# Binding attention matmuls behind the feed-forward column in front of them, in a fused attention and two-layer feed-forward kernel

## The chip, the cores and the metric

The kernel runs on one core of a Trainium2 chip. The metric is the device time of one execution in microseconds (us); lower is better. A core has five engines that run their own instruction queues in order and wait for each other through semaphores: TensorE (PE, matrix products; its weight loads are listed as PEld), VectorE (DVE), ScalarE (ACT), GpSimd (POOL) and SyncE (SP). SP and POOL here mostly issue DMA transfers.

## The reference, cut to what matters

Attention with a memory term over 4 batches, 8 heads, 576 positions of 64, then two feed-forward (FFN) layers over the 2304 tokens, 512 to 2048 to 512 each, all in float32:

```python
scores = q @ k.T / 8, causal          # per batch and head
local  = softmax(scores) @ v
mem    = (phi(q) @ M_prev) / (phi(q) @ z_prev + 1e-6)      # phi(x) = elu(x) + 1
x = g * mem + (1 - g) * local         # g from beta, heads joined: 2304 x 512
x = softplus(x @ w1_in) @ w1_out      # layer 0
x = elu(x @ w2_in) @ w2_out           # layer 1
```

## The kernel before, in words

**FFN.** The 2304 tokens are cut into five chunks of 512, 512, 448, 416 and 416 (`CHUNKS`), each made of parts of one or two batches. `ffn(c, layer)` handles one chunk in one layer, as a generator with 32 yields. Its first half, the in half, makes 16 columns of 128 hidden units: 12 matmuls each (L675 to L677: four slices of the model width, each with a high and a low part of weights and input), then a chain of ScalarE and VectorE instructions (`act`, L679, L680) that ends in a tile g with a high and a low part. Four PSUM banks (tag h) hold columns whose chain is not yet done. Its second half, the out half, makes 4 output tiles in 4 quarters each: 16 steps of 12 matmuls (L691 to L693) that read the g tiles. I write (c, layer) for such a stage, so (1,0) is chunk 1 in layer 0; a stage has 384 matmuls of its own. "Column" below also means a quarter of the out half.

**Attention.** `attention(b, part)` is a generator too. Part A covers positions 0 to 255 of a batch (two heads at once), part B the rest (head by head). A head of part B goes through scores (L344, L356), the maximum (DVE L333), the exponential (ACT L337), scaling (ACT L384), transposes through the PE (L410, and L302 for the memory term), copies that split them into high and low parts (ACT L420, DVE L421), and the gather, a chain of matmuls into one bank (L453, L457, L459, L460). L453 stands once per head, so the L453s count the heads; there are 32 heads in part B. A chunk of FFN can only start when its batches' attention is done.

**Weights.** All four weight matrices arrive in 64-bit form and are converted on the chip (`convert`): a raw load into a buffer of tag big (three of them, shared with the head loads qk of attention), ACT L605, DVE L606 and L607, ACT L97, DVE L616, and a save to DRAM (L584), from where later chunks load them (L635). The generator `conversions` does part of those of layer 1 ahead of time; the rest are made when the column that needs them first comes up. The first use of the output weights of layer 1 is in the out half of (0,1).

**What sets the order.** `TUNE["order"]` lists the stages. For each it has two pairs, for the in half and for the out half: how many attention steps and how many conversions are called per column. `next(side)` calls one attention step, inside `tc.high_priority(offset=400)`. A scheduler then sorts all instructions by priority and by a timeline that it models, under their dependencies, and fixes the order on each engine when the kernel is built. With the high priority it may place the instructions of a step ahead of columns that were called before that step. The loop with `next(side, None)` at L786 to L791 is where the change is made.

Of the kernel before, what the change touches and what calls it, by code (L numbers as in the profile page):

```python
# [18 lines left out]
KD = DM // 128  # L19
KF = DFF // 128  # L20
# [19 lines left out]
    hi='ssss ssss', lo='v', sc='vv ssv',  # L40


    order=((0, 0, (1.6, 0.0), (0.6, 0.2)), (1, 0, (0.1, 0.2), (0.5, 0.6)), (0, 1, (0.7, 0.0), (0.8, 0.0)), (1, 1, (0.8, 0.0), (1.1, 0.0)), (2, 0, (0.3, 0.0), (0.8, 0.0)), (2, 1, (0.5, 0.0), (0.8, 0.0)), (3, 0, (0.3, 0.0), (0.8, 0.0)), (3, 1, (0.5, 0.0), (0.8, 0.0)), (4, 0, (0.0, 0.0), (0.0, 0.0)), (4, 1, (0.0, 0.0), (0.0, 0.0))),
)


# [12 lines left out]
def kernel(  # L59
# [15 lines left out]
    ve, se, ge, te = nc.vector, nc.scalar, nc.gpsimd, nc.tensor  # L75
# [16 lines left out]
    def f32(ap):  # L92
        return ap.bitcast(F32)

    def copy(eng, dst, src):
        if eng is se:
            se.copy(dst, src)  # L97
        else:
            eng.tensor_copy(dst, src)
# [37 lines left out]
    def x(c, k):  # L137
        return slots[SLOT[c]][k]
# [2 lines left out]
        for t in sph:  # L141
            ge.memset(t[:, SOFF[4] + S:], 0.0)

    gates = []
    busy = [set() for _ in CHUNKS]

    def into(b, k, c0, src):
# [474 lines left out]
    def weights(src, key):  # L622
        if key in made:
            w = made.pop(key)
            with tc.issue_after(raw_loads[count - 1]):
                save(key, w)
        else:
            with tc.high_priority(offset=T["pri"][key in scratch]):
                w = make(src, key)
        return w[:, 0], w[:, 1]  # L630
# [18 lines left out]
    def act(c, layer, t, h):  # L649
        if layer == 0:  # L650
            se.activation(t, h, ACTF.Abs)
            se.activation(t, t, ACTF.Exp, scale=-1.0)
            se.activation(t, t, ACTF.Ln, bias=ones)  # L653
            ve.scalar_tensor_tensor(t, h, 0.0, t, ALU.max, ALU.add)  # L654
        elif c == 0:
            se.activation(t, h, ACTF.Relu, scale=-1.0)
            se.activation(t, t, ACTF.Exp, scale=-1.0)
            ve.scalar_tensor_tensor(t, t, -1.0, h, ALU.add, ALU.max)
        else:
            ve.tensor_scalar(t, h, 0.0, None, ALU.min)  # L660
            se.activation(t, t, ACTF.Exp)  # L661
            ve.scalar_tensor_tensor(t, t, -1.0, h, ALU.add, ALU.max)  # L662

    def ffn(c, layer):
        win, wout = ((w1i, w1o), (w2i, w2o))[layer]
        N = WIDTH[c]
        gs = []
        for f in range(KF):
            hi, lo = weights(win[f], f"{layer}i{f}")
            t = two.tile([128, 512], F32, name="t", tag="t")  # L670
            g = gp.tile([128, 2, 512], F32R, name="g", tag="g")
            h = psf.tile([128, 512], F32, name="h", tag="h")
            for k in range(KD):
                xk = x(c, k)
                te.matmul(h[:, :N], hi[:, k, :], xk[:, 0, :N], start=k == 0, stop=False)  # L675
                te.matmul(h[:, :N], hi[:, k, :], xk[:, 1, :N], start=False, stop=False)  # L676
                te.matmul(h[:, :N], lo[:, k, :], xk[:, 0, :N], start=False, stop=k == KD - 1)  # L677
            act(c, layer, t[:, :N], h[:, :N])
            se.copy(g[:, 0, :N], t[:, :N])  # L679
            ve.tensor_sub(g[:, 1, :N], t[:, :N], f32(g)[:, 0, :N])  # L680
            gs.append(g)
            if layer and f == KF - 1:
                busy[c].add("in")
            yield
        for d in range(KD):
            h = psf.tile([128, 512], F32, name="h", tag="h")
            for u in range(4):
                hi, lo = weights(wout[d, u], f"{layer}o{d}_{u}")
                for k in range(4):
                    f = 4 * u + k  # L690
                    te.matmul(h[:, :N], hi[:, k, :], gs[f][:, 0, :N], start=f == 0, stop=False)  # L691
                    te.matmul(h[:, :N], hi[:, k, :], gs[f][:, 1, :N], start=False, stop=False)  # L692
                    te.matmul(h[:, :N], lo[:, k, :], gs[f][:, 0, :N], start=False, stop=f == KF - 1)  # L693
                if u < 3:
                    yield
            if layer == 0:
                y = x(c, d)
                se.copy(y[:, 0, :N], h[:, :N])
                ve.tensor_sub(y[:, 1, :N], h[:, :N], f32(y)[:, 0, :N])
            else:  # L700
                o = two.tile([128, 512], F32, name="t", tag="t")
                copy(se, o[:, :N], h[:, :N])
                at = 0
                for b, c0, n in CHUNKS[c]:
                    nc.sync.dma_start(out[b, d, :, c0:c0 + n], o[:, at:at + n])
                    at += n
            yield
# [36 lines left out]
    with tc.tile_pool(name="pre", bufs=1) as pre, tc.tile_pool(name="pre3", bufs=2) as pre3:  # L744
# [3 lines left out]
        k = 0  # L748
# [29 lines left out]
    for c, layer, *halves in T["order"]:  # L778
        while layer == 0 and not all((b, "A" if c0 < CA else "B") in ready for b, c0, _ in CHUNKS[c]):
            next(side)  # L780
        owed = due = 0.0
        for n, _ in enumerate(ffn(c, layer)):
            share, more = halves[n // KF]
            owed += share
            while owed >= 1.0:
                owed -= 1.0  # L786
                with tc.high_priority(offset=400):
                    next(side, None)
            due += more
            while due >= 1.0:  # L790
                due -= 1.0  # L791
                next(convs, None)
# [72 lines left out]
```

## Time and profile before

| | |
|---|---|
| median of 3 runs | 1066.84 us (1064.32 to 1070.24) |
| profiled execution | 1067.04 us, span of its records 1065.2 us |
| instructions recorded | 15817 |
| PE busy | 96% of the span |
| DVE, ACT busy | 62%, 62% |
| POOL busy | 10% |
| DMA | 248.13 MB, 233 GB/s on average |

The stages lie like this in the trace (start of their first to start of their last matmul): (0,0) 64 to 193 us, (1,0) 193 to 331, (0,1) 331 to 427, (1,1) 428 to 547, (2,0) 547 to 657, (2,1) 657 to 762, (3,0) 762 to 844, then (3,1), (4,0) and (4,1) to the end. The last attention instructions of the PE lie near 800 us. Before 64 us the PE works on attention of part A alone.

Busy time of the PE is no measure of pace: a matmul's record is longer than the distance to the next matmul's start, so that waiting can hide in it. The count of matmuls in a stretch of time tells more.

### The profile page before, as it was taken

To read this page: it belongs to the slowest core of one execution; us is meant where nothing else is said; L and a number is where in the kernel's file an instruction comes from. 1 tells how busy PE (TensorE), PEld (TensorE's weight loads), DVE (VectorE), ACT (ScalarE), POOL (GpSimd) and SP (SyncE) were. 2 spreads that over 40 slices of the span, in tenths; PEclk is the share of its full clock that TensorE was granted. 3 is DMA by queue.
4 is the path that set the end of the run, shared out by engine and by line. 5 is a ranking of instruction groups with operands and counts; after the bars stand their busy time and mean duration, and the time that the engine had idled before them with its cause. 6 is when DMAs were issued, how large, how long until landed. Compare 5 with 4: busy or idle time off the path is not lost.

```text
span 1065.2 us, 15817 instructions
## 1 busy us (share of the span) xinstructions
PE 1018.0 (96%) x5249; PEld 901.8 (85%) x5249; DVE 660.4 (62%) x1684; ACT 664.3 (62%) x1506; POOL 102.4 (10%) x198
## 2 busy tenths in 40 slices
PE   5589999987999999999999999999999999999998
PEld 4467777775888888888889889989999999999998
DVE  5956788798765576897658865992563171240540
ACT  5859976798846666676679965773694141480330
POOL 6013221201100001011111100100000000000000
PEclk9999999998999999999999999999999999999999
DMA  8692599888864599666666555746556678877775
GB/s 237 217 373 54 176 312 319 339 309 297 283 238 164 193 339 347 207 219 214 210 203 224 186 194 190 255 154 215 176 181 221 213 251 247 253 238 230 230 236 176
DMA packets 73345, 248.13 MB, mean 233 GB/s; under 512 B 10528, under 2 KB 15792, under 8 KB 73264
## 3 DMA queue, kind: packets, MB, share of 16 engines
q1 hardware_dynamic: 64432, 215.51, 60.0%
q0 software_dynamic: 8832, 31.61, 9.5%
q8 instruction: 42, 0.69, 0.3%
q14 instruction: 39, 0.32, 0.1%
HBM read 208.81 MB, written 38.27 MB: 232 GB/s over the span
## 4 chain that ended last, share of the span: by engine, by line
PE 81%; DMA 8%; DVE 5%; ACT 5%; issue 1%; SPq 0%; POOL 0%; ACTq 0%; POOLq 0%; DVEq 0%
PE h L692 12%; PE h L691 12%; PE h L693 12%; PE h L675 11%; PE h L677 11%; PE h L676 11%; DMA w<-in_w1i 3%; PE tp L410 3%; PE o L457 2%; PE s L344 2%; DMA w<-in_w2i 2%; DMA w<-s_0o 1%; DMA s_1i<-w 1%; PE o L476 1%; PE s L356 1%
## 5 line engine op out<-in xcount | busy, mean ns | idle before, releaser
L675 PE MATMUL h<-x,w 128*128 128x512 f32 (+2 forms) x640 | 239.3, 378 | 6.4 <-DVE t L654 5.4
L676 PE MATMUL h<-x,w 128*128 128x512 f32 (+2 forms) x640 | 240.3, 375 | 0.0
L677 PE MATMUL h<-x,w 128*128 128x512 f32 (+2 forms) x640 | 239.8, 375 | 0.0
L691 PE MATMUL h<-g,w 128*128 128x512 f32 (+2 forms) x640 | 238.1, 374 | 1.1 <-DMA w<-s_0o 1.1
L692 PE MATMUL h<-g,w 128*128 128x512 f32 (+2 forms) x640 | 238.4, 373 | 0.0
L693 PE MATMUL h<-g,w 128*128 128x512 f32 (+2 forms) x640 | 238.1, 373 | 0.0
L675 PEld LDWEIGHTS h<-x,w 128*128 128x128 f32 x640 | 121.1, 190 | 21.9 <-DVE t L654 7.5
L677 PEld LDWEIGHTS h<-x,w 128*128 128x128 f32 x640 | 121.1, 189 | 13.4
L676 PEld LDWEIGHTS h<-x,w 128*128 128x128 f32 x640 | 121.3, 190 | 13.0 <-issue 0.3
L691 PEld LDWEIGHTS h<-g,w 128*128 128x128 f32 x640 | 120.3, 188 | 13.8 <-DMA w<-s_0o 1.9
L693 PEld LDWEIGHTS h<-g,w 128*128 128x128 f32 x640 | 120.3, 188 | 12.2 <-issue 0.6
L692 PEld LDWEIGHTS h<-g,w 128*128 128x128 f32 x640 | 120.3, 188 | 12.0 <-issue 0.4
L680 DVE TENSOR_TENSOR g<-t,g 128x512 fp32r<-128x512 f32 (+2 forms) x160 | 100.4, 633 | 30.7 <-ACT g L679 29.6
L679 ACT CAST g<-t 128x512 fp32r<-128x512 f32 (+2 forms) x160 | 91.1, 573 | 26.1 <-DVE t L662 17.0
L337 ACT ACTIVATE sph<-sph,neg 128x512 f32<-128x512 f32 (+4 forms) x144 | 83.4, 580 | 25.9 <-DVE neg L333 25.5
L654 DVE SCALAR_TENSOR_TENSOR t<-h,t 128x512 f32<-128x512 f32 (+2 forms) x80 | 50.5, 635 | 64.4 <-ACT t L653 64.0
L333 DVE CUSTOM_DVE_ANT_0 sph<-s,mask 128x384 f32<-128x384 f32 (+3 forms) x112 | 56.5, 519 | 44.3 <-PE s L344 33.0
L410 PE MATMUL tp<-ident,sph 128*128 128x128 f32 x400 | 68.9, 283 | 10.4 <-ACT pt L417 4.8
L605 ACT ACTIVATE wr<-w 128x512 f32<-128x512 f32 x64 | 42.7, 667 | 44.4 <-DMA w<-in_w1i 12.6
L410 PEld LDWEIGHTS tp<-ident,sph 128*128 128x128 f32 x400 | 51.5, 146 | 18.5 <-ACT pt L417 5.2
L421 DVE TENSOR_TENSOR ptj<-tp,ptj 128x512 fp32r<-128x512 f32 (+2 forms) x80 | 40.4, 513 | 40.9 <-ACT ptj L420 30.7
L661 ACT ACTIVATE t<-t 128x416 f32<-128x416 f32 (+2 forms) x64 | 36.7, 579 | 36.3 <-DVE t L660 36.2
(134 smaller groups left out, 1485.9 us busy)
## 6 DMA issues: line engine op xcount, KB each, us to landing
w<-s_1i SPq DMA_DIRECT2D x79, 512.0 KB, 4.1
w<-s_0i SPq DMA_DIRECT2D x64, 512.0 KB, 4.3
w<-s_0o SPq DMA_DIRECT2D x64, 512.0 KB, 3.9
w<-s_1o SPq DMA_DIRECT2D x64, 512.0 KB, 4.3
w<-in_w1i SPq DMA_DIRECT2D x16, 512.0 KB, 5.3
s_0i<-w SPq DMA_DIRECT2D x16, 512.0 KB, 8.9
w<-in_w1o SPq DMA_DIRECT2D x16, 512.0 KB, 5.7
w<-in_w2i SPq DMA_DIRECT2D x16, 512.0 KB, 5.4
```

Of the source, the lines that this page charges most:

```text
L333: ve.tensor_tensor_reduce(out=dst, in0=ps, in1=m, scale=-0.125, scalar=least, op0=ALU.add, op1=ALU.min, accum_out=acc)
L337: se.activation(Pi, Pi, ACTF.Exp, scale=-1.0, bias=d["neg", n][:, i:i + 1], accum_out=sums(n, i))
L410: te.transpose(pt, sph[n % 2][:, poff(n, i) + 128 * j:poff(n, i) + 128 * j + 128], ident)
L654: ve.scalar_tensor_tensor(t, h, 0.0, t, ALU.max, ALU.add)
L675: te.matmul(h[:, :N], hi[:, k, :], xk[:, 0, :N], start=k == 0, stop=False)
L676: te.matmul(h[:, :N], hi[:, k, :], xk[:, 1, :N], start=False, stop=False)
L677: te.matmul(h[:, :N], lo[:, k, :], xk[:, 0, :N], start=False, stop=k == KD - 1)
L679: se.copy(g[:, 0, :N], t[:, :N])
L680: ve.tensor_sub(g[:, 1, :N], t[:, :N], f32(g)[:, 0, :N])
L691: te.matmul(h[:, :N], hi[:, k, :], gs[f][:, 0, :N], start=f == 0, stop=False)
L692: te.matmul(h[:, :N], hi[:, k, :], gs[f][:, 1, :N], start=False, stop=False)
L693: te.matmul(h[:, :N], lo[:, k, :], gs[f][:, 0, :N], start=False, stop=f == KF - 1)
```

## The change

Two things. First, `ffn` notes the last matmul of each column in `column`, and from the second stage of the list on, each attention step is called inside `tc.issue_after(column[0])`. This adds an ordering edge from that matmul to each TensorE instruction of the step, and to those alone: it is no wait at run time, since both are on the PE's queue, but the scheduler can no longer place them ahead of the end of the column that was called before the step. The steps' instructions on the other engines and their DMAs get no edge. Second, the numbers of steps per column are set anew.

```diff
-order=((0, 0, (1.6, 0.0), (0.6, 0.2)), (1, 0, (0.1, 0.2), (0.5, 0.6)), (0, 1, (0.7, 0.0), (0.8, 0.0)), (1, 1, (0.8, 0.0), (1.1, 0.0)), (2, 0, (0.3, 0.0), (0.8, 0.0)), (2, 1, (0.5, 0.0), (0.8, 0.0)), (3, 0, (0.3, 0.0), (0.8, 0.0)), (3, 1, (0.5, 0.0), (0.8, 0.0)), ...
+order=((0, 0, (1.6, 0.0), (0.6, 0.2)), (1, 0, (0.1, 0.2), (0.25, 0.6)), (0, 1, (0.8, 0.0), (1.0, 0.0)), (1, 1, (0.8, 0.0), (1.0, 0.0)), (2, 0, (0.3, 0.0), (0.8, 0.0)), (2, 1, (0.4, 0.0), (0.7, 0.0)), (3, 0, (0.3, 0.0), (0.8, 0.0)), (3, 1, (0.4, 0.0), (0.7, 0.0)), ...
...
-                te.matmul(h[:, :N], lo[:, k, :], xk[:, 0, :N], start=False, stop=k == KD - 1)
+                end = te.matmul(h[:, :N], lo[:, k, :], xk[:, 0, :N], start=False, stop=k == KD - 1)
+            column[:] = [end.ins]
...
-                    te.matmul(h[:, :N], lo[:, k, :], gs[f][:, 0, :N], start=False, stop=f == KF - 1)
+                    end = te.matmul(h[:, :N], lo[:, k, :], gs[f][:, 0, :N], start=False, stop=f == KF - 1)
+                column[:] = [end.ins]
...
-                with tc.high_priority(offset=400):
+                with tc.high_priority(offset=400), tc.issue_after(column[0]) if c or layer else nullcontext():
                     next(side, None)
```

Lines behind the first added one carry numbers higher by one or two in the changed kernel (L680 for L679, L692 to L694 for L691 to L693); the attention's lines keep theirs.

The order of the PE up to the end of (0,0) is the same in both kernels. From (1,0) on, the PE's rows of attention (all rows that are not L675 to L677 or L691 to L693; each repeat counts) fall on the stages so:

| | (1,0) in, out | (0,1) in, out | (1,1) in, out | (2,0) in, out | (2,1) in, out | (3,0) in, out | (3,1) in, out |
|---|---|---|---|---|---|---|---|
| before | 131, 83 | 31, 26 | 102, 116 | 116, 96 | 109, 63 | 68, 0 | 0, 0 |
| after | 17, 27 | 101, 94 | 104, 112 | 53, 101 | 58, 65 | 43, 98 | 58, 10 |

The PE in the in half of (1,0), between the end of the fourth column (tile h_2206) and the fifth (h_2229), before:

```order
L677 MATMUL h_2206<-x1_3_105,w_2202 128x512
L410 MATMUL tp_2679<-ident_89,sph0_96 128x128 x4
L302 MATMUL tp_2686<-ident_89,e_2123 128x128 x3
L410 MATMUL tp_2746<-ident_89,sph0_96 128x128 x4
L410 MATMUL tp_2756<-ident_89,sph0_96 128x128 x4
L453 MATMUL o_2807<-phi_2690,ms_2696 128x320
L410 MATMUL tp_2877<-ident_89,sph1_97 128x128 x4
L675 MATMUL h_2229<-x1_0_102,w_2225 128x512
```

The same place in the changed kernel:

```order
L676 MATMUL h_2183<-x1_3_105,w_2179 128x512
L677 MATMUL h_2183<-x1_3_105,w_2179 128x512
L676 MATMUL h_2206<-x1_3_105,w_2202 128x512
L677 MATMUL h_2206<-x1_3_105,w_2202 128x512
L675 MATMUL h_2229<-x1_0_102,w_2225 128x512
```

Here 20 attention matmuls (transposes into four PSUM tiles tp and the start of a gather o) are gone; they come later, behind columns of (0,1).

The PE in the in half of (0,1), within the fifteenth column (weights 1i14), before:

```order
L675 MATMUL h_3600<-x0_2_100,w_3596 128x512
L676 MATMUL h_3600<-x0_2_100,w_3596 128x512
L677 MATMUL h_3600<-x0_2_100,w_3596 128x512
L675 MATMUL h_3600<-x0_3_101,w_3596 128x512
L676 MATMUL h_3600<-x0_3_101,w_3596 128x512
```

and in the changed kernel:

```order
L676 MATMUL h_3544<-x0_2_100,w_3540 128x512
L453 MATMUL o_3521<-phi_3273,ms_3284 128x320
L457 MATMUL o_3521<-ptj_2093,vs_3287 128x320 x3
L344 MATMUL s_3511<-R_3371 128x512
L344 MATMUL s_3511<-R_3371,QL_3372 128x512
L457 MATMUL o_3521<-ptj_2093,vs_3287 128x320 x3
L677 MATMUL h_3544<-x0_2_100,w_3540 128x512
```

A gather and scores of the next head now stand where there was no attention.

ScalarE in the out half of (0,1), about its second output copy (t from h; eight quarters of 16 are done by then), before:

```order
L605 ACTIVATE wr_4132<-w64_4133 128x512
L97 CAST w_4066<-wr_4067 128x512
L605 ACTIVATE wr_4175<-w64_4176 128x512
L97 CAST w_4108<-wr_4109 128x512
L97 CAST w_4131<-wr_4132 128x512
L97 COPY t_4005<-h_3860 128x512
```

and in the changed kernel:

```order
L97 CAST w_4053<-wr_4054 128x512
L420 CAST ptl_2094<-tp_3795 128x128
L605 ACTIVATE wr_4090<-w64_4091 128x512
L337 ACTIVATE sph0_96,sm_3846<-sph0_96,neg_3847 128x384
L605 ACTIVATE wr_4132<-w64_4133 128x512
L337 ACTIVATE sph1_97,sm_3846<-sph1_97,neg_3848 128x384
L97 COPY t_3973<-h_3822 128x512
```

The conversion steps (L605, L97 into w) are now mixed with attention, and the second copy comes behind the casts of 10 of the 16 output weight tiles where it came behind 12; the third copy comes behind 13 where it came behind 14.

## Rows read from the trace of the kernel before

**Rows 1.** Page, busy time, share of the span and instructions of each engine

```profile
PE 1018.0 (96%) x5249; PEld 901.8 (85%) x5249; DVE 660.4 (62%) x1684; ACT 664.3 (62%) x1506; POOL 102.4 (10%) x198
```

**Rows 2.** Stretches: length, busy us (instructions) per engine, PEclk, DMA share, GB/s

```profile
350.00:375.00 25.00, 25.00 (x109) 20.11 (x108) 13.90 (x22) 17.78 (x31) 0.00 (x0) 1.00 0.58 194
850.00:875.00 25.00, 25.00 (x134) 24.57 (x133) 19.80 (x37) 13.29 (x25) 0.00 (x0) 1.00 0.79 252
427.50:547.00 119.50, 119.50 (x613) 101.78 (x612) 89.58 (x229) 76.84 (x186) 10.77 (x21) 1.00 0.62 203
```

**Rows 3.** Stretches as before; engines in the order PE, PEld, DVE, ACT, POOL

```profile
64.00:132.00 68.00, 65.17 (x330) 49.87 (x329) 42.65 (x126) 53.97 (x124) 16.94 (x31) 0.97 0.50 170
193.00:276.00 83.00, 72.33 (x342) 57.19 (x340) 72.28 (x171) 74.90 (x163) 13.95 (x27) 0.94 0.86 305
276.00:427.50 151.50, 151.25 (x716) 125.21 (x715) 97.51 (x213) 97.66 (x196) 8.99 (x18) 1.00 0.74 260
547.00:604.50 57.50, 56.06 (x315) 51.85 (x314) 46.32 (x125) 55.91 (x134) 6.57 (x12) 1.00 0.62 209
547.00:657.00 110.00, 107.71 (x604) 99.81 (x603) 80.31 (x216) 90.38 (x217) 12.97 (x24) 1.00 0.65 215
657.00:714.50 57.50, 55.85 (x309) 51.03 (x308) 52.13 (x137) 43.83 (x103) 5.34 (x10) 1.00 0.57 191
657.00:844.00 187.00, 185.35 (x1019) 175.76 (x1018) 104.31 (x265) 110.68 (x256) 5.34 (x10) 1.00 0.60 198
```

**Rows 4.** Waits of the PE from 193 to 276 us: total, times, longest

```profile
PE tp L410 <- DVE ptj L421: 2.8, 1, 2.8
PE o L457 <- ACT ptj L420: 2.3, 1, 2.3
```

**Rows 5.** ScalarE groups, shapes apart: busy us, mean ns, idle time before

```profile
L605 ACT ACTIVATE wr<-w 128x512 f32<-128x512 f32 x64 | 42.7, 667 | 44.4 <-DMA w<-in_w1i 12.6 <-DMA w<-in_w2i 9.5 <-DMA w<-in_w1o 9.0
L679 ACT CAST g<-t 128x512 fp32r<-128x512 f32 x64 | 39.2, 615 | 9.2 <-DVE t L658 6.8 <-DVE t L662 1.8
L97 ACT CAST w<-wr 128x512 fp32r<-128x512 f32 x64 | 39.0, 614 | 7.5 <-PE h L693 3.0 <-PE h L677 1.7 <-issue 1.6
L653 ACT ACTIVATE t<-t,ones 128x512 f32<-128x512 f32 x32 | 22.8, 719 | 0.1
L652 ACT ACTIVATE t<-t 128x512 f32<-128x512 f32 x32 | 19.9, 628 | 0.2
L651 ACT ACTIVATE t<-h 128x512 f32<-128x512 f32 x32 | 18.6, 587 | 3.6 <-PE h L677 2.4 <-DVE g L680 1.2
L657 ACT ACTIVATE t<-t 128x512 f32<-128x512 f32 x16 | 10.1, 634 | 0.3
L661 ACT ACTIVATE t<-t 128x512 f32<-128x512 f32 x16 | 10.1, 633 | 2.9 <-DVE t L660 2.9
L656 ACT ACTIVATE t<-h 128x512 f32<-128x512 f32 x16 | 9.5, 596 | 3.8 <-PE h L677 3.8
```

**Rows 6.** VectorE groups, shapes apart: busy us, mean ns, idle time before

```profile
L616 DVE TENSOR_TENSOR w<-wr,w 128x512 fp32r<-128x512 f32 x64 | 43.9, 686 | 5.4 <-ACT w L97 5.1
L607 DVE SCALAR_TENSOR_TENSOR wr<-w,wr 128x512 int32<-128x512 int32 x64 | 43.9, 686 | 0.8
L680 DVE TENSOR_TENSOR g<-t,g 128x512 fp32r<-128x512 f32 x64 | 43.7, 686 | 9.8 <-ACT g L679 9.4
L606 DVE TENSOR_SCALAR wr<-wr 128x512 int32<-128x512 int32 x64 | 27.3, 426 | 29.5 <-ACT wr L605 29.3
L660 DVE TENSOR_SCALAR t<-h 128x512 f32<-128x512 f32 x16 | 11.0, 686 | 0.6 <-PE h L677 0.4
L662 DVE SCALAR_TENSOR_TENSOR t<-t,h 128x512 f32<-128x512 f32 x16 | 10.8, 678 | 1.1 <-ACT t L661 1.0
```

**Rows 7.** DMA issues by line: KB each, median us to landing

```profile
w<-in_w2o SPq DMA_DIRECT2D x16, 512.0 KB, 5.3
```

**Rows 8.** Waits of all engines from 380 to 428 us: total, times, longest

```profile
POOL qk L195 <- DMA s_1o<-w: 46.7, 1, 46.7
```

More of the change, by code (lines that the diff above doesn't have):

```diff
@@ L40 @@
     hi='ssss ssss', lo='v', sc='vv ssv',
-    order=((0, 0, (1.6, 0.0), (0.6, 0.2)), (1, 0, (0.1, 0.2), (0.5, 0.6)), (0, 1, (0.7, 0.0), (0.8, 0.0)), (1, 1, (0.8, 0.0), (1.1, 0.0)), (2, 0, (0.3, 0.0), (0.8, 0.0)), (2, 1, (0.5, 0.0), (0.8, 0.0)), (3, 0, (0.3, 0.0), (0.8, 0.0)), (3, 1, (0.5, 0.0), (0.8, 0.0)), (4, 0, (0.0, 0.0), (0.0, 0.0)), (4, 1, (0.0, 0.0), (0.0, 0.0))),
+    order=((0, 0, (1.6, 0.0), (0.6, 0.2)), (1, 0, (0.1, 0.2), (0.25, 0.6)), (0, 1, (0.8, 0.0), (1.0, 0.0)), (1, 1, (0.8, 0.0), (1.0, 0.0)), (2, 0, (0.3, 0.0), (0.8, 0.0)), (2, 1, (0.4, 0.0), (0.7, 0.0)), (3, 0, (0.3, 0.0), (0.8, 0.0)), (3, 1, (0.4, 0.0), (0.7, 0.0)), (4, 0, (0.0, 0.0), (0.0, 0.0)), (4, 1, (0.0, 0.0), (0.0, 0.0))),
 )
@@ L142, in pads @@
             ge.memset(t[:, SOFF[4] + S:], 0.0)
-    gates = []
+    gates, column = [], []
     busy = [set() for _ in CHUNKS]
```

## The prediction

> **What bounds the kernel now.** I read the page's busy times first. The PE shows 96% of the span, DVE and ACT 62% each [rows 1], so the PE bounds the kernel as a whole; but its records overlap, and waiting hides in them. So next I read the table of stretches, and counted matmuls. Where nothing but FFN of 512 columns runs, 109 matmuls start in 25 us: 0.2294 us each. With 416 columns it is 134: 0.1866 us. Both are 0.448 ns per column, so 448 columns take 0.2007 us. Stage (1,1) has a PE busy throughout: 119.5 us with 613 matmuls, of which 384 are its FFN at 0.2294, 88.1 us. The other 31.4 us are 229 attention matmuls, 0.137 us each [rows 2]. With these two paces every stretch can be priced and set against its length [rows 3]:
>
> - (0,0), in half: 192 FFN are 44.0 us, 138 attention 18.9; 62.9 against 68.0, so 5.1 lost. The change leaves this half as it is.
> - (1,0), in half, 193 to 276 us: 44.0 and 150 times 0.137, 20.6; 64.6 against 83.0, so 18.4 lost.
> - the rest of (1,0) and all of (0,1), 276 to 427.5: 132.1 and 19.2; 151.3 against 151.5, 0.2 lost.
> - (2,0): 77.1 and 220 times 0.137, 30.1; 107.2 against 110.0, 2.8 lost, of which the in half has 2.1 (38.5 and 16.9 against 57.5).
> - (2,1) to (3,0): 77.1, 71.6 and 251 times 0.137, 34.4; 183.1 against 187.0, 3.9 lost, of which the in half of (2,1) has 3.0 (38.5 and 16.0 against 57.5).
>
> From 193 us on 25.3 us are lost, and 18.4 of them lie in one half stage. There the PE's longest waits are for copies that free or fill the transposes' tiles, on DVE and on ACT [rows 4], and both of these engines are busy for 72.3 and 74.9 of 83.0 us [rows 3]. That half is bound by ACT and DVE. The granted clock there is 0.94, the mean of its two levels 1.2 and 2.4 GHz, so 0.12 of the stretch ran at the lower one and half of that, 5.0 us, is lost to it; in the in halves of (2,0) and (2,1), with 2.1 and 3.0 us lost, it stays at 1.00.
>
> The Trainium skill (Perfetto Trace Analysis, Identifying the Most-Contended Engine) says that matmul busy time tells little of how close TensorE is to its limit, and that the busy share of weight loads tells more. The trace bears out the first half: 96% goes with these losses. By the second half, (1,0)'s in half with 57.19 of 83.0 us against 125.21 of 151.5 in the next stretch would have lost 83.0 times (1 - 0.689/0.826), 13.8 us, not 18.4, and the forecast below would be 4.6 us higher, near 1060; I go by the count, since the mix of matmuls differs between the two.
>
> **The change part by part.** The total of the work stays: each instruction of attention, FFN and conversion is still there, and the edge is none at run time. What changes is where attention lies. By the two orders, (1,0) goes from 131 and 83 attention rows on the PE to 17 and 27, (0,1) from 31 and 26 to 101 and 94; (1,1) hardly changes, and what was in (2,0) and (2,1) spreads to the end of (3,1). The 941 rows of the order from (1,0) on are 990 records in the trace (150, 140, 229, 220 and 251), 1.05 per row.
>
> What a matmul of attention brings to the other engines follows from (1,1), which has no conversions. ACT was busy 76.84 us; 16 columns of 0.633 and 0.615 are 20.0 [rows 5]; 56.8 over 229 is 0.248 us. DVE was busy 89.58; 16 columns of 0.686, 0.678 and 0.686 are 32.8 [rows 6]; that is 0.248 too. One conversion costs ACT 0.667 and 0.614, 1.28 us, and DVE 0.426, 0.686 and 0.686, 1.80 us [rows 5, 6].
>
> (1,0), in half. Before, ACT had 16 columns of 0.587, 0.628, 0.719 and 0.615 (40.8 us), by its order 11 conversions (14.1) and 131 rows' worth of attention (138 times 0.248, 34.2): 89 us against 62.9 of the PE, a ratio of 1.42. DVE had 22.0, 10 conversions (18.0) and 34.2: 74 us, 1.18. After, ACT has 40.8, 4 conversions (5.1) and 18 times 0.248 (4.5): 50.4 us against 44.0 and 2.5, 46.5 of the PE, 1.08. DVE has 34 us, 0.72. The nearest row for one engine somewhat over the PE with the other free is the in half of (2,0): ACT 35.7 (40.8 times 448/512) and 122 times 0.248, together 66.0 against 55.4, 1.19, DVE 0.89, and 2.1 us lost. I take 2.5 us in place of 18.4; the out half behind it leaves ACT time to catch up.
>
> (0,1). It takes the moved work together with the first conversions of the output weights, which I count from its order: 5 in the in half, 12 in the out half. In half: PE 44.0 and 106 times 0.137, 58.5. ACT 16 times 0.596, 0.634 and 0.615 (29.5), 6.4 and 26.3: 62.2, ratio 1.06. DVE 22, 9.0 and 26.3: 57.3, 0.98. Bounds for it are the in half of (2,1) (DVE 28.7 and 28.4 against 54.6, 1.05; ACT 0.84; 3.0 lost) and that of (1,0) before (18.4 lost). Its ratios are near the first, but both engines are tight, so I take 5. Out half: PE 57.6, DVE 21.6 and 24.6, 46.2, ratio 0.80; ACT 0.7. I take 1.5. Today (0,1) loses nearly nothing, so this is what comes in late in place of the stall that goes.
>
> The rest. (1,1) with 104 and 112 rows in place of 102 and 116: 0.5. (2,0): the in half has ACT 35.7 and 13.9 against 46.2 of the PE, 1.07: 1.5. At its start the sixteenth gather, on which the fourth input slice hangs, now stands behind the first columns: nine FFN matmuls (1.8 us) cover four instructions on ACT and DVE, which by the shortest and longest rows [rows 5, 6] take 1.7 to 2.9 us, so 0 to 1.1 late; I take 1.0. Its out half 0.5. (2,1) to (3,1), thinner everywhere: 1.0. The sum is 2.5 + 6.5 + 0.5 + 3.0 + 1.0 = 13.5 us lost in place of 25.3: 11.8 us gained. The profiled execution took 1067.04 us, 0.2 over the median of the runs, so no correction is needed: 1055 us.
>
> The attention's end moves from about 800 us into the out half of (3,1), where its last gather stands 14 columns (31 us) ahead of (4,0), which needs it. That is enough cover; if it were used up, the delay would be added in full.
>
> **The rivals.** *The stall moves, whole (no change).* (0,1) could behave as (1,0) did: for the stage as a whole DVE has 103.5 and ACT 102.1 (output copies left out) of 116.1 us, both 0.9, and conversions and attention alternate on in-order queues. If it loses 18.4 in place of 6.5, the time is 1055 + 11.9, 1067. Against it: the ratios of its in half are 1.06 and 0.98, not 1.42 and 1.18. The Trainium skill (TensorE: Matmul & The Clock Gate, Part 1: The HAM clock gate) has it that an idle array falls back to half its rate; the trace agrees in (1,0) with 0.94. Without such a fall the same waits would cost 13.4 there, and this rival 1062.
>
> *Weights come late (slower).* The out half of (0,1) needs one converted tile per quarter of 3.6 us. A conversion holds one of three big buffers for its landing, 5.3 us [rows 7], and 3.1 us of ACT and DVE work: 8.4 us. Heads of attention use the same buffers, and a head's load has waited 46.7 us for one here [rows 8]. In the changed order the lead on ACT is 2 tiles at the second output copy, not 4, and 1 at the third, not 2. If for six tiles two buffers hold heads, each tile comes 4.8 us late: 28.8 us, 1084. It decides from some four such tiles. Against it: today the same conversions run there in a shorter stage that loses nothing (151.3 against 151.5), and the head's wait shows that conversions get the buffers first.
>
> *Nothing is left of the stalls.* If ACT and DVE always run far enough ahead, all 25.3 us go: 1042. For it: no half stage is left with a ratio over 1.1. Against it: halves with 1.05 to 1.2 on one engine lost 2 to 3 us each.
>
> **How the numbers follow.** Forecast 0.50, with an own range of 1050 to 1062 (8 to 20 us lost); stall moved 0.25; weights late 0.12; nothing left 0.13. A measurement of this kernel tells about 0.5% from no change, here 1061.5 to 1072.2. Faster: 0.47 of the forecast, 0.13, and 0.03 of the moved stall, 0.63. Same: 0.03 and 0.21, 0.24. Slower: 0.13. The range goes from 1042, the last rival, to 1070, which holds most of the moved stall and leaves out the late weights.
>
> **What would show it.** In the new profile the in half of (1,0) should take 48 to 51 us in place of 83, its clock should be 1.00, and the PE's waits for ptj there should be gone. (0,1) should take 119 to 126 us with DVE and ACT busy around 85%. Wrong would be: over 130 us for (0,1), with waits of the PE for ptj or for w made from in_w2o; a wait over 2 us for x at the start of (2,0); or a gap before (4,0).

## The result and the profile after

| | before | changed | changed, again on another chip |
|---|---|---|---|
| median (range) of the runs, us | 1066.88 (1064.32 to 1072.81) | 1057.71 (1053.53 to 1062.78) | 1059.51 (1055.08 to 1063.02) |
| ratio to before, 95% interval | | 0.9906 [0.9879, 0.9934] | 0.9935 [0.991, 0.996] |
| profiled execution, us | 1067.04 | 1058.49 | 1055.08 |

The ratios are gains of 10.0 us (7.0 to 12.9) and 6.9 us (4.3 to 9.6). The forecast was 1055 us, a gain of 11.8: inside the first interval, above the second.

The busy times of the page say as little as before: the PE has 1012.6 us (96% of the span), 5.4 us less than in [rows 1], and DVE and ACT 63% each.

The table of stretches of the changed kernel, cut at its own stage starts: length, busy us (instructions) of PE, PEld, DVE, ACT, POOL, the granted clock, DMA share, GB/s. In order: (1,0) in and out; (0,1) in and out; (1,1); (2,0) in and out; (2,1) with (3,0); (3,1).

```profile
189.70:243.20 53.50, 49.91 (x219) 39.15 (x218) 32.66 (x60) 43.20 (x79) 6.29 (x13) 0.97 0.87 306
243.20:294.30 51.10, 49.27 (x221) 40.59 (x220) 27.94 (x60) 24.88 (x48) 2.66 (x5) 0.97 0.87 316
294.30:353.40 59.10, 59.10 (x299) 49.96 (x298) 44.84 (x105) 47.79 (x106) 4.29 (x8) 1.00 0.58 200
353.40:417.40 64.00, 61.48 (x310) 50.80 (x309) 54.84 (x141) 50.62 (x116) 6.95 (x13) 1.00 0.89 310
417.40:532.90 115.50, 115.50 (x591) 97.90 (x590) 90.46 (x229) 77.41 (x179) 13.24 (x24) 1.00 0.64 216
532.90:584.30 51.40, 48.56 (x249) 44.28 (x248) 30.72 (x73) 43.40 (x95) 3.20 (x6) 0.97 0.59 201
584.30:638.40 54.10, 54.10 (x304) 50.46 (x303) 34.24 (x94) 35.15 (x84) 5.03 (x10) 1.00 0.57 196
638.40:824.50 186.10, 186.10 (x1039) 177.91 (x1038) 118.47 (x288) 119.16 (x276) 10.47 (x19) 1.00 0.64 215
824.50:906.30 81.80, 81.80 (x456) 80.86 (x455) 39.47 (x94) 32.19 (x75) 0.00 (x0) 1.00 0.64 210
```

Each row is priced as the prediction priced [rows 3]: 192 FFN matmuls per half at the chunk's pace, the others at 0.137 us, and the rest of the length is lost. The in half of (1,0): 192 times 0.2294 and 27 times 0.137 are 47.7, of 53.5, so 5.8 lost. The same sums for the second profiled execution of this kernel (its table by the same cuts is not shown, but for the first row of it below) stand in the last column. All losses are us; by one or two records that a trace misses they are uncertain by some tenths.

| | before | forecast | after | after, again |
|---|---|---|---|---|
| (1,0) in | 18.4 | 2.5 | 5.8 | 3.2 |
| (1,0) out | } 0.2 | 0 | 3.1 | 1.4 |
| (0,1) in | } | 5 | 0.4 | 0.4 |
| (0,1) out | } | 1.5 | 3.8 | 3.5 |
| (1,1) | 0 | 0.5 | -1.0 | -1.0 |
| (2,0) in | 2.1 | 2.5 | 5.1 | 5.0 |
| (2,0) out | 0.7 | 0.5 | 0.2 | 0.2 |
| (2,1) to (3,1) | 3.9 | 1.0 | 0.5 | 0.5 |
| sum | 25.3 | 13.5 | 17.9 | 13.2 |

By the rows, then, 7.4 and 12.1 us come from where the change acts. The profiled span fell by 8.5 and 11.9 us; (1,0) began 3.1 and 0.7 us earlier than before, which is no effect of the change, since the PE's order up to there is the same. That leaves 5.4 and 11.2 us from the start of (1,0) on, 2.0 and 0.9 us less than the rows give. The 1.0 that (1,1) takes less than its price shows the size of error that one mean price for all attention matmuls brings. Before and after are single executions, and the runs of one kernel lie up to 9 us apart.

**Where the 5.8 us of (1,0) come from.** Waits of the PE from 189 to 245 us (waiting instruction, releaser, total us, times, longest):

```profile
PE h L675 <- DMA w<-s_0i: 3.6, 2, 3.4
```

The waits for ptj of [rows 4] are gone. What stands there now is seen in the timeline of the PE (start, length, instruction, idle time before it in brackets) and, behind it, of SP's DMA issues:

```profile
201.15 1.09 PE L675 MATMUL h<-x,w 128*128 128x512 f32 x4
...
203.71 0.40 PE L677 MATMUL h<-x,w 128*128 128x512 f32 x1
207.50 0.47 PE L675 MATMUL h<-x,w 128*128 128x512 f32 x1 [3.39 <-DMA w<-s_0i]
```

```profile
202.74 1.91 SPq L635 DMA_DIRECT2D w<-s_0i  x4
```

Four L675 in one row are the fourth input slice of four columns: the first four columns had all waited for it, with all four PSUM banks of tag h and all four weight tiles. From the first matmul on that slice to the last it is 2.6 us (201.15 to 203.71), so the weight tiles come free close together, the next four loads are issued in a row from 202.74 on, and the fifth column waits 3.39 us. Right behind it the clock falls (a stretch of the same table):

```profile
210.00:215.00 5.00, 5.00 (x19) 3.94 (x18) 2.60 (x4) 3.04 (x6) 0.00 (x0) 0.76 0.97 374
```

I call this a bunch. The change did not make it: the kernel before has the same one, and behind it, from 209.26 on, the 20 attention matmuls that the order shows between the fourth and the fifth column:

```profile
206.47 1.09 PE L675 MATMUL h<-x,w 128*128 128x512 f32 x4
...
213.46 0.66 PE L410 MATMUL tp<-ident,sph 128*128 128x128 f32 x4 [2.84 <-DVE ptj L421]
...
216.03 0.79 PE L675 MATMUL h<-x,w 128*128 128x512 f32 x1
```

There the four loads are issued from 208.06 on, and the fifth column starts 8.0 us later without a wait for them: the attention, with a wait of its own, covered them. In the changed kernel it starts 4.8 us after the first load was issued. With the attention gone, the wait for the loads shows.

In the repeated execution the same column waits at the same place for another thing, the chain that frees the bank, and the clock stays up; a row of its table and one of its PE timeline:

```profile
192.20:243.10 50.90, 48.14 (x219) 38.09 (x218) 33.16 (x61) 43.12 (x79) 6.35 (x13) 1.00 0.89 316
```

```profile
208.81 0.48 PE L675 MATMUL h<-x,w 128*128 128x512 f32 x1 [2.76 <-DVE t L654]
```

**The 3.1 us of (1,0)'s out half** hold one wait, for weights loaded back from DRAM, and a clock of 0.97. The same wait is in the repeated execution, where the clock stays at 1.00 and the half loses 1.4:

```profile
PE h L692 <- DMA w<-s_0o: 1.8, 1, 1.8
```

**(2,0) starts with a bunch too.** The PE's timeline of the changed kernel there:

```profile
544.07 0.97 PE L675 MATMUL h<-x,w 128*128 128x448 f32 x4
...
546.29 0.36 PE L677 MATMUL h<-x,w 128*128 128x448 f32 x1
...
550.26 0.66 PE L675 MATMUL h<-x,w 128*128 128x448 f32 x1 [2.67 <-DVE sm L397]
```

The sixteenth gather stands behind the first columns, as the order said; the four columns end together, and the fifth waits 2.67 us. The engine named is the last that the profile saw, on DVE's queue. That the chain that frees the bank lies behind it is inferred: ACT is busy for 4.52 of the 5 us from 545 on, and DVE's t L654, a step of that chain, waits 3.9 us there for ACT's L653.

**The out half of (0,1).** The PE's waits from 353 to 418 us:

```profile
PE h L692 <- ACT w L97: 1.4, 3, 1.0
PE h L694 <- DVE w L616: 0.6, 1, 0.6
```

Output weights being converted come late, in small: 2.0 us, the rival called "weights come late" without its size. 1.25 us of it stand at the start of the fourth and the fifth of the 16 quarters (364.53 and 369.06), ahead of the output copies at which the prediction counted the lead; 0.75 stand at 407.45 and 409.08. DVE was busy 44.84 us in the in half and 54.84 in this one, where the prediction counted 57.3 and 46.2 by the order: part of the work counted in the first half ran in the second. ACT's 47.79 in the in half against 62.2 counted say the same.

### The profile page after: what moved, and what is told of

The parts are those of the page before. It is cut to its first block, busy times and chain, and to the rows that moved or that the text cites. A ratio compares the mean times of both kernels' runs of the same rounds, so it can differ in the third digit from the quotient of the medians.

```text
span 1056.7 us, 15834 instructions
## 1 busy us (share of the span) xinstructions
PE 1012.6 (96%) x5249; PEld 898.9 (85%) x5249; DVE 662.6 (63%) x1684; ACT 667.6 (63%) x1506; POOL 102.5 (10%) x198
## 3 DMA queue, kind: packets, MB, share of 16 engines
HBM read 208.81 MB, written 38.27 MB: 234 GB/s over the span
## 4 chain that ended last, share of the span: by engine, by line
PE 78%; DMA 10%; ACT 6%; DVE 4%; issue 1%; SPq 1%; ACTq 0%; DVEq 0%
PE h L675 11%; PE h L692 11%; PE h L676 11%; PE h L693 11%; PE h L694 11%; PE h L677 11%; DMA w<-in_w2o 3%; PE tp L410 3%; DMA w<-in_w1i 2%; PE o L457 2%; PE s L344 2%; DMA w<-s_0i 1%; PE s L356 1%; DMA w<-in_w1o 1%; PE o L476 1%
## 5 line engine op out<-in xcount | busy, mean ns | idle before, releaser
L675 PE MATMUL h<-x,w 128*128 128x512 f32 (+2 forms) x640 | 238.5, 379 | 9.3 <-DMA w<-s_0i 3.6
L692 PE MATMUL h<-g,w 128*128 128x512 f32 (+2 forms) x640 | 239.0, 375 | 3.5 <-DMA w<-s_0o 1.8
L677 PE MATMUL h<-x,w 128*128 128x512 f32 (+2 forms) x640 | 239.7, 374 | 0.0
L694 PE MATMUL h<-g,w 128*128 128x512 f32 (+2 forms) x640 | 238.3, 373 | 0.6 <-DVE w L616 0.6
L693 PE MATMUL h<-g,w 128*128 128x512 f32 (+2 forms) x640 | 238.8, 374 | 0.0
L675 PEld LDWEIGHTS h<-x,w 128*128 128x128 f32 x640 | 120.9, 189 | 24.5 <-DVE t L654 6.9
L692 PEld LDWEIGHTS h<-g,w 128*128 128x128 f32 x640 | 120.7, 189 | 15.8 <-DMA w<-s_0o 2.1
L677 PEld LDWEIGHTS h<-x,w 128*128 128x128 f32 x640 | 121.1, 189 | 12.9
L694 PEld LDWEIGHTS h<-g,w 128*128 128x128 f32 x640 | 120.7, 189 | 13.4 <-DVE w L616 1.3
L676 PEld LDWEIGHTS h<-x,w 128*128 128x128 f32 x640 | 121.2, 189 | 12.5 <-issue 0.3
L693 PEld LDWEIGHTS h<-g,w 128*128 128x128 f32 x640 | 120.6, 188 | 11.9 <-issue 0.4
L680 ACT CAST g<-t 128x512 fp32r<-128x512 f32 (+2 forms) x160 | 91.3, 573 | 24.9 <-DVE t L662 20.8
L337 ACT ACTIVATE sph<-sph,neg 128x256 f32<-128x256 f32 (+4 forms) x144 | 83.4, 581 | 31.2 <-DVE neg L333 30.8
L654 DVE SCALAR_TENSOR_TENSOR t<-h,t 128x512 f32<-128x512 f32 (+2 forms) x80 | 50.1, 636 | 66.6 <-ACT t L653 66.6
L333 DVE CUSTOM_DVE_ANT_0 sph<-s,mask 128x256 f32<-128x256 f32 (+3 forms) x112 | 56.4, 519 | 43.4 <-PE s L344 31.8
L605 ACT ACTIVATE wr<-w 128x512 f32<-128x512 f32 x64 | 42.9, 671 | 51.4 <-DMA w<-in_w2i 22.6
L410 PE MATMUL tp<-ident,sph 128*128 128x128 f32 x400 | 62.3, 279 | 7.0 <-ACT pt L417 6.9
L410 PEld LDWEIGHTS tp<-ident,sph 128*128 128x128 f32 x400 | 49.9, 144 | 14.8 <-ACT pt L417 7.1
```

The source lines that it names most:

```text
L333: ve.tensor_tensor_reduce(out=dst, in0=ps, in1=m, scale=-0.125, scalar=least, op0=ALU.add, op1=ALU.min, accum_out=acc)
L337: se.activation(Pi, Pi, ACTF.Exp, scale=-1.0, bias=d["neg", n][:, i:i + 1], accum_out=sums(n, i))
L410: te.transpose(pt, sph[n % 2][:, poff(n, i) + 128 * j:poff(n, i) + 128 * j + 128], ident)
L677: end = te.matmul(h[:, :N], lo[:, k, :], xk[:, 0, :N], start=False, stop=k == KD - 1)
L694: end = te.matmul(h[:, :N], lo[:, k, :], gs[f][:, 0, :N], start=False, stop=f == KF - 1)
```

## The experiments

Each is a change of one of the two kernels, timed against the kernel before on the same chip; where not said otherwise in five rounds. Losses are worked out from the rows as above. In the texts on record the theories have letters: A is that the binding brings the gain by taking attention out of (1,0)'s in half, A1 that it does so because ScalarE and VectorE are overloaded there, A2 that it is the PE's order and not that load; C, that the binding is also needed in later stages; D, that the late sixteenth gather costs (2,0) its loss; E, that in (1,0) the weight loads are late even without the bunch.

**e1_table.** The kernel before with the new numbers of steps, without the binding.

> The kernel before with the new numbers of steps, without the binding. Theory A (the edges move attention out of the in half of (1,0), and that is the gain): the built order still has 129 attention rows there (131 before, 17 in the changed kernel), so that half still takes about 83 us and the time stays at 1063 to 1069 us. Rival B (the new numbers of steps bring the gain, the edges little): 1055 to 1060 us.

Median 1059.96 us, ratio 0.9937 [0.9913, 0.9961]. In halves of (1,0) and (2,1), from its table of stretches:

```profile
191.20:272.70 81.50, 69.12 (x334) 55.48 (x334) 68.25 (x162) 72.26 (x158) 10.82 (x22) 0.94 0.85 297
655.10:705.70 50.60, 50.60 (x277) 47.18 (x276) 43.26 (x108) 37.06 (x86) 3.74 (x7) 1.00 0.61 200
```

(1,0) still takes 81.5 us with 142 attention matmuls and loses 18.0: with the priority that the steps have, a smaller number of steps does not move them out of it; the binding does. But the time is a miss for A and lies in the range of rival B: with the stall of 18.0 us still there, this kernel gains 5.8 us by the medians, and its ratio is nearly that of the repeated changed kernel (0.9935). 2.5 of the gain is (2,1), which loses 0.4 in place of 3.0 [rows 3]. The rest I can't place: its profiled execution was the slowest of its runs (1063.84), and from the start of (1,0) on it is only 1.3 us shorter than before.

**e2_bind.** The binding alone, with the numbers of before.

> The binding with the old numbers of steps. Theory A: the in half of (1,0) has 17 rows in this order too and takes about 53 us as in the changed kernel; the out half has 62 rows in place of 27 and gives (0,1) fewer (77 and 97); 1055 to 1060 us. Rival B (the new numbers are needed): 1064 us or more.

Median 1059.93, ratio 0.9936 [0.9914, 0.9958]. In half of (1,0); (0,1) and its out half alone; in half of (2,0); and the PE's wait at the start of (2,0):

```profile
191.10:246.50 55.40, 49.84 (x218) 39.18 (x217) 30.31 (x55) 40.74 (x74) 6.10 (x13) 0.97 0.82 284
299.90:413.70 113.80, 113.80 (x573) 96.26 (x572) 95.58 (x229) 93.70 (x205) 11.50 (x22) 1.00 0.81 282
355.20:413.70 58.50, 58.50 (x300) 50.02 (x299) 50.43 (x127) 45.47 (x105) 7.08 (x13) 1.00 0.91 322
528.60:585.80 57.20, 50.58 (x267) 46.56 (x266) 35.31 (x84) 48.75 (x107) 3.19 (x6) 0.94 0.54 179
```

```profile
PE h L675 <- DVE t L654: 6.2, 1, 6.2
```

The in half of (1,0) loses 7.8 with 26 attention matmuls, so the binding alone takes most of its stall away, as A said. (0,1) loses nothing (189 attention matmuls: 114.0), but (2,0) loses 8.4. Each part alone gives some 6 us by the medians and both together 7 to 10, and the intervals of e1_table, e2_bind and the repeated changed kernel lie on each other. So the times do not show that the second part adds to the first; what each does is seen by place, in the rows.

**e4_bind10.** The changed kernel, bound in (1,0) only.

```diff
-                with tc.high_priority(offset=400), tc.issue_after(column[0]) if c or layer else nullcontext():
+                with tc.high_priority(offset=400), tc.issue_after(column[0]) if (c, layer) == (1, 0) else nullcontext():
```

> The changed kernel with the binding in stage (1,0) alone; all later stages are free to place their steps early again. Theory A, narrow form (only the in half of (1,0) matters): that half has 17 rows and takes about 53 us, total 1054 to 1061 us. Rival C (the binding is also what keeps the later stages, (2,0) above all with 154 rows in its in half here in place of 53, from stalling): (2,0)'s in half loses over 8 us and the total is 1063 to 1072 us.

Median 1061.65, ratio 0.9959 [0.994, 0.9979]. The in halves of (1,0) and (2,0):

```profile
192.60:245.70 53.10, 49.63 (x219) 39.21 (x218) 32.22 (x59) 42.27 (x78) 6.24 (x13) 0.97 0.86 297
531.00:602.60 71.60, 66.25 (x354) 59.45 (x353) 52.69 (x146) 63.97 (x153) 6.39 (x12) 0.95 0.51 169
```

Unbound, attention gathers in (2,0) as it did in (1,0): 162 matmuls, 10.9 lost in place of 5.1, with 2.7 us in one wait of a transpose (L410) for its scaled scores (DVE L386). That the binding is needed there too (C) holds by this place, at 5.8 us; the time is a near miss for both, above A's range and below C's, and some 4 us of the gain are kept.

**x_act4.** The changed kernel with four more ScalarE instructions behind each column of (1,0)'s in half; three rounds. Their output is not used.

```diff
...
+            if (c, layer) == (1, 0):
+                for _ in range(4):
+                    se.activation(spare, f32(g)[:, 0, :], ACTF.Identity, bias=ones)
...
+    spare = const.tile([128, 512], F32, name="spare")
```

> The changed kernel with four more ScalarE instructions of 0.6 us behind each column of (1,0) in layer 0, which write a tile that nobody reads; the PE's order is unchanged. 38 of the 64 stand before that half's last cast, so ScalarE has about 50 + 24 = 74 us of work there against 46 us of the PE. Theory A1 (the work of ScalarE and VectorE in that half is what stalled the PE before): the half takes 65 us or more in place of 53, total 1068 to 1080 us. Rival A2 (what stalled it was attention matmuls standing in the PE's queue ahead of columns, waiting for copies; load alone does little): the half takes under 57 us, total under 1063 us.

Median 1076.72, ratio 1.0089 [1.0058, 1.0121]. The in half, and the PE's longest wait in it:

```profile
192.40:262.60 70.20, 52.14 (x218) 39.75 (x216) 34.62 (x62) 59.68 (x110) 6.31 (x13) 0.95 0.74 255
```

```profile
PE h L675 <- DVE t L654: 11.7, 4, 4.7
```

22.6 us lost with 26 attention matmuls: load on ACT alone is enough for a stall of this size, and A2 falls as it was written. But it is not the old stall over again. Here the PE waits for the chain that frees a column's bank; in the kernel before 7.8 of its 10.6 us of waits in this half were at transposes and gathers (the longest in [rows 4]), and this order has taken nearly all of those out of the half.

**x_noconv.** The kernel before without conversions in (1,0), which then come when they are first needed.

```diff
-    order=(..., (1, 0, (0.1, 0.2), (0.5, 0.6)), ...),
+    order=(..., (1, 0, (0.1, 0.0), (0.5, 0.0)), ...),
```

> The kernel before without conversions called in (1,0); they fall on (0,1). The in half of (1,0) keeps 127 of its 131 attention rows on the PE, but ScalarE has 76.5 us of work there in place of 88 and VectorE 60 in place of 74 (summed over the built order), against 63 us of the PE. Theory A1 (load of both engines): the half loses 5 to 12 us in place of 19. Rival A2 (attention matmuls standing in the PE's queue ahead of columns, whatever the load): it loses 16 us or more.

Median 1067.81, ratio 1.0006 [0.9984, 1.0028]. In halves of (1,0), (0,1) and (2,0):

```profile
191.90:264.70 72.80, 68.17 (x336) 55.77 (x335) 56.77 (x144) 67.01 (x149) 8.60 (x18) 0.95 0.60 206
315.90:373.70 57.80, 52.41 (x230) 41.82 (x228) 50.53 (x102) 50.40 (x98) 2.13 (x4) 0.97 0.85 294
540.80:612.50 71.70, 65.02 (x357) 58.39 (x356) 55.77 (x153) 67.48 (x158) 9.53 (x17) 0.98 0.55 187
```

With nearly the same attention (144 matmuls for 150) and less load, (1,0) loses 9.0 in place of 18.4, as A1 said: about half of the stall goes with the conversions. Whether the other half is load or the place of the transposes these runs do not tell. (0,1), to which the conversions went, now loses 8.6, and (2,0), which has none but 165 attention matmuls in place of 123, 10.5; the time is that of before.

**v01_early_a.** The changed kernel with more steps in (0,0), so that the input slices of (1,0) are there sooner: `(0, 0, (1.8, 0.0), ...)` for 1.6.

> The changed kernel with 1.8 in place of 1.6 attention steps per column in the in half of (0,0). The last gather of part A then stands ahead of the first column of (1,0); in the changed kernel it stands inside the third, and the first four columns wait together for the fourth input slice. Theory D (this bunch of columns, which hold all four weight buffers and end together, is what the 6 us lost in the in half of (1,0) are): that half loses under 3 us, its wait for w loaded from s_0i is gone. Rival E (the weight load is late for the DMA's sake, whatever the order): the wait stays and 5 us or more are lost.

Median 1065.12, ratio 0.9982 [0.9962, 1.0001]. Out half of (0,0), in half of (1,0), out half of (0,1); then the PE's waits in the second:

```profile
130.90:201.50 70.60, 67.65 (x346) 50.79 (x345) 53.56 (x156) 45.93 (x113) 16.29 (x31) 1.00 0.84 287
201.50:251.70 50.20, 47.35 (x200) 37.61 (x198) 39.75 (x79) 47.13 (x88) 1.07 (x2) 0.97 0.91 337
358.00:429.20 71.20, 64.98 (x312) 53.41 (x313) 60.49 (x153) 52.44 (x122) 9.66 (x18) 0.93 0.83 287
```

```profile
PE h L675 <- DMA w<-s_0i: 2.4, 1, 2.4
PE h L675 <- ACT x L152: 1.5, 1, 1.5
```

A miss, and for (1,0) D falls: its columns now end one after another (the last matmuls of three of them start at 203.99, 206.78 and 209.58), and it still loses 5.1, with a wait of 2.4 us for a weight tile at 212.39 behind which the clock falls (E, in part), and one for an input slice that is late all the same. The out half of (0,0) loses 5.4, and the out half of (0,1) 10.7, with 120 attention matmuls where the changed kernel has 118 and loses 3.8: their count alone does not decide there. Most of it is in one place: at 417.87 transposes have waited 4.9 us for their scaled scores (ACT L384), and the clock of 0.93, reckoned as in the prediction, is worth up to 5.0.

**z3_early_b.** The changed kernel with steps moved up so that the sixteenth gather is done before (2,0): `(0, 1, (0.9, 0.0), (1.1, 0.0))` for 0.8 and 1.0.

> The changed kernel with 0.9 and 1.1 in place of 0.8 and 1.0 steps per column in (0,1). The gather that (2,0) hangs on then stands ahead of (2,0) in the PE's order, and its first columns run one after another. Theory D: the in half of (2,0) loses under 2.5 us in place of 5.2. At the same time the out half of (0,1) has 131 attention rows in place of 94 beside the same 12 conversions. If late weights bound that half (5.1 us lost in the changed kernel), it should lose more, 6 to 12 us; if they do not, about 5. Total 1052 to 1062 us.

Median 1065.56, ratio 0.9997 [0.9975, 1.0018]. Out half of (0,1), in half of (2,0), and the PE's waits in the first:

```profile
352.70:431.60 78.90, 68.95 (x328) 56.77 (x328) 65.72 (x169) 58.79 (x134) 10.16 (x19) 0.91 0.81 275
550.90:596.80 45.90, 45.90 (x246) 42.72 (x245) 31.65 (x70) 42.10 (x95) 3.19 (x6) 1.00 0.65 215
```

```profile
PE tp L410 <- ACT sph L384: 4.0, 1, 4.0
PE tp L410 <- DVE sph L386: 3.6, 1, 3.6
```

(2,0) loses nothing once the gather is early: D holds there. In v01_early_a (0.1 lost), w1_both (none) and the y runs below (0.9 and 1.0) the attention steps stand earlier too; in the four profiles with the gather late (the changed kernel twice, e2_bind, c1_convs) it loses 5 to 10. But the out half of (0,1), which loses 3.8 with 118 attention matmuls, loses 16.2 with 136: its two longest waits are at transposes as in (1,0) before, and this is the "stall moves" rival as it was written.

**w1_both.** Both corrections, with the steps for (2,0) taken into (1,1): `(0, 0, (1.8, 0.0), ...)` and `(1, 1, (1.0, 0.0), (1.2, 0.0))`.

> The changed kernel with 1.8 steps per column in the in half of (0,0) and 1.0 and 1.2 in (1,1). Both bunches are gone in the built order, at the start of (1,0) and of (2,0). Theory D: (1,0) in and (2,0) in lose under 3 and 2.5 us; with the rest as in the changed kernel 1049 to 1055 us. Rival E: 1056 us or more. The in half of (2,0) has 92 rows in place of 53.

Median 1065.84, ratio 0.9988 [0.9967, 1.001]: a miss. (2,0) loses nothing again, but (1,0)'s in half loses 4.5, not under 3, with 2.3 us of waits for weights from s_0i, and the out half of (0,1), with the same change in (0,0) as v01_early_a and the same wait of 4.9 us, loses 11.2 (71.7 us with 120).

**after_again** is the changed kernel, to have it on one chip with the next ones.

> The changed kernel once more, beside the three below on one chip: 1053 to 1063 us as in its first runs.

1059.51, as in the first table.

**c1_convs.** The changed kernel with six more conversions called in the out half of (1,0), so that (0,1) has fewer: `(1, 0, (0.1, 0.2), (0.25, 1.0))` for 0.6.

> The changed kernel with 1.0 in place of 0.6 conversions per column in the out half of (1,0). By its order 7 conversions stand in the out half of (0,1) in place of 12; VectorE has 44 us of work there in place of 59, ScalarE 38 in place of 54, with the same 96 attention rows on the PE (94). Theory A1 (load of ScalarE and VectorE bounds that half too): it loses under 2 us in place of 5.1, total 2 to 4 us below the changed kernel. Rival (the transposes' order, not the load): 4 us or more lost, total unchanged.

Median 1054.94 (1054.63 to 1055.37, four runs), ratio 0.9894 [0.9867, 0.9921]. Out halves of (1,0) and (0,1), in half of (2,0):

```profile
244.50:291.90 47.40, 47.39 (x220) 39.54 (x221) 29.69 (x62) 26.99 (x51) 2.13 (x4) 1.00 0.93 339
350.40:407.20 56.80, 56.80 (x293) 48.40 (x292) 43.97 (x111) 41.02 (x90) 6.94 (x13) 1.00 0.84 291
524.90:582.50 57.60, 53.03 (x259) 46.24 (x258) 35.06 (x86) 46.20 (x104) 3.73 (x7) 0.94 0.59 198
```

By its four runs it is the fastest version: 4.6 us below the changed kernel on the same chip by the medians (2 to 4 expected), though the two intervals overlap a little. Its profile does not show where: the profiled executions of both took 1055.08 us. The out half of (0,1) loses nothing, as A1 said, with 43.97 us of work on DVE in place of 54.84. But fewer conversions there also mean that tiles are ready earlier, and load alone does not decide in this half: e2_bind loses nothing with DVE busy 50.43 and ACT 45.47 us. The start of (2,0) got worse (9.9 lost), with the bunch still in it.

**y1_spread and y2_spread** take load off (0,1) by its attention, which moves ahead into (1,0) and behind into (1,1), with the sixteenth gather in time for (2,0). The changed kernel with (y1)

```diff
-    order=(..., (1, 0, (0.1, 0.2), (0.25, 0.6)), (0, 1, (0.8, 0.0), (1.0, 0.0)), (1, 1, (0.8, 0.0), (1.0, 0.0)), ...),
+    order=(..., (1, 0, (0.1, 0.2), (0.9, 0.6)), (0, 1, (0.6, 0.0), (0.8, 0.0)), (1, 1, (0.8, 0.0), (1.1, 0.0)), ...),
```

and, in y2, `(1, 0, (0.2, 0.2), (0.75, 0.6))`.

> The changed kernel with 0.9 steps per column in the out half of (1,0), 0.6 and 0.8 in (0,1), 0.8 and 1.1 in (1,1). By its order the out half of (1,0) has 90 attention rows in place of 27, (0,1) 179 in place of 195, and the gather that (2,0) hangs on comes early enough that its columns run one after another. Theories A1 and D together: (0,1) loses under 3 us in place of 6.4, the in half of (2,0) under 2 in place of 5.2, the out half of (1,0) under 2 in place of 3.6: 1046 to 1053 us. Rival: the loss moves into (1,0), which conversions share: 1057 us or more.

> The changed kernel with 0.2 and 0.75 steps per column in (1,0), 0.6 and 0.8 in (0,1), 0.8 and 1.1 in (1,1): 29 and 90 attention rows in (1,0), 167 in (0,1). As the one before, with 12 more rows in the in half of (1,0), where ScalarE already has 50 us of work against 46 of the PE. Theories A1 and D: 1046 to 1053 us, and the in half of (1,0) loses 5 to 8 us.

1063.73, ratio 0.9982 [0.9965, 0.9999], and 1064.64, ratio 0.9983 [0.9968, 0.9999]: both misses. The in half of (2,0) loses 0.9 and 1.0 and the out half of (1,0) nothing and 0.2, as expected, but the in half of (1,0) loses 8.2 and 10.9 (5 to 8 expected for y2). The out half of (0,1) in y1, and its longest wait:

```profile
361.70:428.40 66.70, 60.33 (x288) 48.94 (x286) 48.44 (x118) 41.98 (x95) 8.00 (x15) 0.95 0.83 279
```

```profile
PE h L692 <- ACT w L97: 3.8, 2, 3.2
```

With 96 attention matmuls, five fewer than c1, it loses 9.5 (c1: none), and y2 7.7 with 95. DVE and ACT have 48.44 and 41.98 us of work there, less than in e2_bind, so it is not the load. 3.8 us are waits for converted tiles, 2.4 waits of transposes for scaled scores, and the clock of 0.95, reckoned as before, up to 3.3. What puts the conversions late in y1 and not in c1 and e2_bind was not settled.

## Why the prediction was right, and where not

- **The change takes the stall of (1,0) away.** Right: the half went from 83.0 to 53.5 and 50.9 us, against 48 to 51 said, its clock to 0.97 and 1.00, against 1.00, and the waits for ptj are gone. e1_table keeps the stall with the steps unbound, e2_bind loses most of it with the binding alone.
- **That half is bound by ACT and DVE.** Borne out in part: x_noconv halves the loss by taking load off, and x_act4 makes a stall by load alone, though at another wait. How much of the other half is the place of the transposes on the PE is not shown.
- **The term of 2.5 us for it was too small**: 5.8 and 3.2, and 3.1 and 1.4 more in the out half, where nothing was expected. The ratio of 1.08 on ACT was not where it went: ACT was busy 43.2 us in that half against a price of 47.7 for the PE. 3.4 of the 5.8 us are the wait of the fifth column and some 1.5 the clock behind it. The step that failed is that only the work of ACT and DVE was summed: the weights that (1,0) loads back from DRAM had no term, and they cost waits of 3.6 us in the in half and 1.8 in the out half. The trace of before held the sign, four columns that end together at 206.47 and their loads behind them, covered by the attention that the change takes out. That the bunch is the whole reason is not so: without it (v01_early_a, w1_both) the half lost 5.1 and 4.5, again with waits for weights.
- **(0,1) at 6.5 us**: 4.2 and 3.9; it takes 123.1 us where 122.6 were forecast and 119 to 126 said, with DVE at 81% and ACT at 80% (85% said). But the halves are the other way round: 0.4 in the in half (5 forecast, with ratios of 1.06 and 0.98) and 3.8 in the out half (1.5, with 0.80). The count by the order put 12.5 us more of DVE's work into the in half than the trace has there, and 8.6 less into the out half; and a ratio says nothing of when a converted tile is due, where most of the waits are for w.
- **(2,0) at 3.0**: 5.3 and 5.2. The late gather was named, and priced at 1.0 for a wait for x at the gather itself. That wait did not come (the sign of being wrong was over 2 us of it); the price is the bunch behind it, 2.67 us for the fifth column, and the clock's fall (below). z3_early_b shows the cause.
- **(2,1) to (3,1) at 1.0**: 0.5. Right; e1_table has (2,1)'s part without the binding.
- **The sum**: 13.5 forecast, 17.9 and 13.2 in two executions. That the second comes so near is luck: its terms are off by up to 4.6 us, too much for (0,1)'s in half and too little for (1,0), (0,1)'s out half and (2,0), and these cancel. Of the 4.7 us between the two executions 2.6 lie in (1,0)'s in half and 1.7 in its out half, as much as what separates the forecast from the result.
- **The rivals.** "The stall moves" is what z3_early_b does with 18 more attention matmuls in the out half of (0,1), and v01_early_a in part with two more; the changed kernel stands that near to it. "Weights come late" is there with 2.0 us of waits for converted tiles, and in y1_spread with 3.8; the larger waits for weights, 3.6 and 1.8 us in (1,0), were for reloaded ones, which it did not name. "Nothing is left" was wrong by 13 to 18 us. No gap came before (4,0): (3,1) loses 0.3.

What stays open: where e1_table gains with the stall still in it, and so how much of the change's gain in time is the binding's; why conversions are late in y1_spread and y2_spread; why the scaled scores are late in the out half of (0,1) in v01_early_a and w1_both; and whether the reloaded weights of (1,0) are late by the order of the loads or by the traffic (DMA share 0.87 there).

## What to carry to other kernels

Price each half stage by counts of matmuls and their paces, and look for the one where two other engines have more work than TensorE; move load out of it, and check each half that gets it, since one that loses little can stand close to a stall (3.8 us with 118 attention matmuls, 16.2 with 136). When filler work is taken from the start of a stage, look in the old trace at what it covered: columns that wait for one late input end together and give back their buffers together, and the wait for the next loads shows once the filler is gone. A stage's share of busy time does not tell when a tile is due; read that from the order of the engine that makes it.

## What the runs showed of the hardware

The granted clock did not follow from the length of a wait alone. After an idle time of 3.39 us at 207.50 the first matmuls ran at the high level, and from 208.97 to 212.37 eight of them started 0.425 us apart in place of 0.233, some 1.5 us lost (0.76 for 210 to 215). At 550.26, after 2.67 us, the slow ones came at once. In the repeated execution, after 2.76 us at 208.81, the half stayed at 1.00. The Trainium skill (TensorE: Matmul & The Clock Gate, Part 1: The HAM clock gate) has an idle array fall to half its rate; the trace agrees in the first two places, and in the third no fall follows. In the first place the fall added some 1.5 us to a wait of 3.39, which is part of why the two executions differ there (5.8 and 3.2 us lost).
